# A decode layer that streams its cache: sixteen-row loads, a staggered first chunk of w_down, and a store that all engines wait for

## The chip, the cores and the metric

The program runs on one core of one Trainium2 chip. The time is device time in microseconds of one execution; before the change the median of three runs is 1310.91 us. All profile rows are of one further, profiled execution. In them PE is TensorE, PEld its weight loads, DVE VectorE, ACT ScalarE, POOL GpSimd and SP SyncE; a q behind the name marks the engine's sequencer, which issues the DMAs. Times in rows count from the first instruction.

## What is computed

One token goes through an attention block over a cache of 65,536 positions and then through a bilinear feed-forward block. Everything is float32.

```python
# x (1,1,512); 32 query heads, 8 key/value heads, Dh 128, Sk 65536; F 1792
q = (layernorm(x) @ wq).reshape(32, 128)
p = softmax(q . k_cache[h // 4] * 128 ** -0.5)       # per query head
h = x + concat(p . v_cache[h // 4]) @ wo
hn = layernorm(h)
out = h + ((hn @ w_gate) * (hn @ w_up)) @ w_down
```

K and V are 268 MB each; all weights together are 27.3 MB.

## The kernel before, in words

All work of the engines is written out by hand with semaphores. Two slots in SBUF, `slots[0]` (slot_a) and `slots[1]` (slot_b), of 128 partitions by 64 KiB, take turns. The query weights `wq` (8 MiB) go into slot_a and the first tile of K into slot_b (L107, L108). After that, for each of the eight key/value heads, four tiles of K and four tiles of V of 8 MiB each follow (L130). SP issues each when TensorE has finished with the tile that was two earlier in the same order, which the counter `c_pe` tells it. TensorE multiplies the tiles (L276 for scores, L301 for the weighted sum of V). VectorE and ScalarE do the maximum, the exponentials and the copies out of PSUM.

At the start ACT issues the load of x (L105) into `x_col`, 128 rows of four elements. VectorE normalises it (L176 to L188) with two small sums over partitions on TensorE (L247, L248), and TensorE multiplies it with wq (L255) once slot_a is full. `psm` is a bank of PSUM that these small results share.

At the end the slots receive `wo` in two pieces (L139, slot_b) and w_gate and w_up (L142, L145, slot_a). w_down has a place of its own, `wd_t`, of 128 rows by 14 chunks of 512 elements, 2 KiB a row and chunk. It comes in five loads whose bounds in chunks are `WD_CUTS` (L149), and each has a semaphore. TensorE waits for w_down's pieces in order (L402) and adds four matmuls for each chunk (L407). VectorE then copies the sum into `y` (L411), SP stores four of y's rows, one for each quarter of the output (L412), and SP alone waits for the store (L414). All loads but x's are issued by SP, in the order of the code, without waits of their own between the pieces of w_up and w_down.

Of the kernel before, what the change touches and what calls it, by code (L numbers as in the profile page):

```python
# [15 lines left out]
KT = D // P  # L16
# [7 lines left out]
SMALL = 17408  # L24
SLOT_A, SLOT_B, SLOT_C = 65536, 131072, 196608
WO_CUT = 6 * REP * D
WU_CUTS = (0, 2, 3, 4)
WD_CUTS = (0, 4, 8, 11, 13, 14)


class Counter:
# [8 lines left out]
        return self.n  # L40


def body(nc, xc, kT, v, wq, wo, wg, wu, wd, out):
# [21 lines left out]
    x_col, xd, xq, hq = (sb(n, P, KT) for n in ("x_col", "xd", "xq", "hq"))  # L65
    eps_t, sel_1 = sb("eps_t", P, 1), sb("sel_1", P, 1)
    sel_h, sel_b, sel_q = sb("sel_h", P, REP), sb("sel_b", P, 16), sb("sel_q", P, 4)
    stat = sb("stat", P, 16)
# [17 lines left out]
    pva, psm = ps("pva"), ps("psm")  # L86

    slot_sem = [nc.alloc_semaphore("in_a"), nc.alloc_semaphore("in_b")]
    sem_x, sem_out = nc.alloc_semaphore("in_x"), nc.alloc_semaphore("out")
    tail_sem = [nc.alloc_semaphore(f"in_w{i}") for i in range(12)]  # L90
    dve_pe, act_pe = nc.alloc_semaphore("dve_pe"), nc.alloc_semaphore("act_pe")
    c_pe, c_dve, c_act, c_pool = (Counter(nc, n) for n in ("c_pe", "c_dve", "c_act", "c_pool"))
# [4 lines left out]
        out=ident, in_=ident, compare_op=ALU.not_equal, fill=1.0, base=0,  # L97
# [13 lines left out]
    Q_ROWS, Q_COLS = 3, 5  # L111
    BASE, PER_HEAD = 5, 16
    K_DONE, MT, MB, T_DONE, V_DONE, PL, PO = 1, 5, 6, 7, 11, 15, 16

    def pe_at(h, k):
# [18 lines left out]
    tail = iter(tail_sem)  # L134
    wo_sems, wu_sems, wd_sems = [], [], []
# [10 lines left out]
            wu_sems[-1][1], 16)  # L146
    for lo, hi in zip(WD_CUTS, WD_CUTS[1:]):
        wd_sems.append((lo, next(tail)))
        SP.dma_start(wd_t[:, lo * D:hi * D], wd[:, lo * D:hi * D]).then_inc(wd_sems[-1][1], 16)  # L149


    def dve(ins):
        return c_dve.up(ins)
# [4 lines left out]
    dve(DVE.memset(mean_m, 1.0 / D))  # L158
    dve(DVE.memset(ones, 1.0))
    for t in (pva, psm):  # L160
        dve(DVE.memset(t, 0.0))
# [14 lines left out]
    t = dve(DVE.tensor_reduce(out=s1, in_=x_col, axis=AX.X, op=ALU.add)._wait_ge(sem_x, 16))  # L176
    ln_in = t
    dve(DVE.tensor_copy(x_pad[:, :, 0], x_col))
    t = dve(DVE.tensor_copy(mean, psm[:, 0:1])._wait_ge(c_pe.sem, 1))
# [5 lines left out]
    ln_std = c_act.up(ACT.activation(  # L185
        std, psm[:, 1:2], AF.Sqrt, bias=eps_t[:, 0:1], scale=1.0)._wait_ge(c_pe.sem, 2))
    t = dve(DVE.reciprocal(rstd, std)._wait_ge(c_act.sem, ln_std))
    xn_done = dve(DVE.tensor_scalar(  # L188
        out=xn_pad[:, :, 0], in0=xd, scalar1=rstd, scalar2=None, op0=ALU.mult)._wait_ge(
# [5 lines left out]
    for i in range(2):  # L195
        t = dve(DVE.tensor_copy(
            q_all[:, 4 * i:4 * i + 4, :],
            ptp[i][:, 0:16].rearrange("p (r j) -> p j r", j=4)))
    dve_to_pe(DVE.tensor_copy(q_pad[:, 28:28 + REP], q_all[:, 0, :])._wait_ge(c_dve.sem, t))

    for h in range(HKV):
        for n in range(NT):
            t = dve(DVE.tensor_reduce(  # L203
                out=mx[:, n:n + 1], in_=psc[n], axis=AX.X, op=ALU.max)._wait_ge(
                    c_pe.sem, pe_at(h, K_DONE + n)))
        dve_to_pe(DVE.tensor_reduce(out=m1, in_=mx, axis=AX.X, op=ALU.max)._wait_ge(c_dve.sem, t))
        t = dve(DVE.tensor_reduce(
            out=m_row, in_=psm[0:1, 0:P].rearrange("p (g h) -> p h g", h=REP), axis=AX.X,
            op=ALU.max)._wait_ge(c_pe.sem, pe_at(h, MT)))
# [3 lines left out]
            out=nbias, in0=psm[:, 128:129], scalar1=-SCALE, scalar2=None,  # L213
# [7 lines left out]
        for n in range(NT):  # L221
# [18 lines left out]
    def pe(ins):  # L240
        return c_pe.up(ins)

    def take(sem, n=1):
        PE.sem_inc(sem, -n).wait_op(sem, n, "sem-ge")  # L244

    PE.wait_ge(c_dve.sem, ln_in)
    pe(PE.matmul(psm[:, 0:1], mean_m, s1, start=True, stop=True))  # L247
    pe(PE.matmul(psm[:, 1:2], mean_m, s2, start=True, stop=True)._wait_ge(c_dve.sem, ln_sq))  # L248
    PE.wait_ge(c_dve.sem, xn_done)
    take(slot_sem[0], 16)  # L250
    for i in range(2):
        for k in range(KT):
            for j in range(4):
# [3 lines left out]
                    start=(k == 0), stop=(k == KT - 1))  # L257
    assert pe(ins) == Q_ROWS
    PE.wait_ge(c_dve.sem, q_rows)
    for i in range(2):  # L260
        for r in range(REP):
            ins = PE.matmul(
                ptp[i][:, 4 * r:4 * r + 4], q_row[i][:, r * P:(r + 1) * P], sel_q,
                start=True, stop=True)
        t = pe(ins)
    assert t == Q_COLS == BASE

    with PE.Fori(0, HKV):
        take(dve_pe)
        for n in range(NT):  # L270
# [14 lines left out]
            start=True, stop=True))  # L285
# [113 lines left out]
    wd_at = dict(wd_sems)  # L399
    for c in range(NC):  # L400
        if c in wd_at:
            PE.wait_ge(wd_at[c], 16)  # L402
        if c == 8:
            PE.wait_ge(c_dve.sem, fp1_done)
        for j in range(4):
            o = c * D + j * P
            ins = PE.matmul(  # L407
                pd[32 * j:32 * j + 32, 0:P], f_pad[:, c, :], wd_t[:, o:o + P],
                start=False, stop=(c == NC - 1))
    pd_done = pe(ins)  # L410
    y_done = dve(DVE.tensor_copy(y, pd[:, 0:P])._wait_ge(c_pe.sem, pd_done))  # L411
    SP.dma_start(out, y[0:P:32, :])._wait_ge(  # L412
        c_dve.sem, y_done).then_inc(sem_out, 16)
    SP.wait_ge(sem_out, 16)  # L414


# [32 lines left out]
```

## Time and profile before

| | before |
|---|---|
| median of 3 runs | 1310.91 us (1310.81 to 1310.94) |
| the profiled execution, as timed | 1310.62 us |
| its span, first to last instruction | 1309.3 us |
| mean granted TensorE clock | 0.735 |
| bytes moved by DMA | 564.81 MB, 431 GB/s over the span |
| DMA packets | 11107, of which 1364 under 512 B |
| load of wq, issue to landing | 21.9 us |
| load of x, issue to landing | 12.3 us |

The page gives busy time by engine, 40 equal slices of the span, the DMA queues, the chain of work that ended last, the costliest groups of instructions and the DMA issues. The views behind it give the same for any stretch: windows (busy time of each engine in a stretch, then TensorE's clock, the busy share of the 16 DMA engines and GB/s, where a packet is booked whole where it starts), the timeline, the waits, and the DMA of one stretch. A share over 1 in a short window comes from that booking.

### The profile page before, as it was taken

To read this page: it belongs to the slowest core of one execution; us is meant where nothing else is said; L and a number is where in the kernel's file an instruction comes from. 1 tells how busy PE (TensorE), PEld (TensorE's weight loads), DVE (VectorE), ACT (ScalarE), POOL (GpSimd) and SP (SyncE) were. 2 spreads that over 40 slices of the span, in tenths; PEclk is the share of its full clock that TensorE was granted. 3 is DMA by queue.
4 is the path that set the end of the run, shared out by engine and by line. 5 is a ranking of instruction groups with operands and counts; after the bars stand their busy time and mean duration, and the time that the engine had idled before them with its cause. 6 is when DMAs were issued, how large, how long until landed. Compare 5 with 4: busy or idle time off the path is not lost. (4 is left out here: it accounts for less than half of the span.)

```text
span 1309.3 us, 9941 instructions
## 1 busy us (share of the span) xinstructions
PE 669.7 (51%) x4692; PEld 201.7 (15%) x4692; DVE 69.2 (5%) x177; ACT 28.0 (2%) x72; POOL 2.6 (0%) x13
## 2 busy tenths in 40 slices
PE   3447445455535534554543654555464554456357
PEld 1112011121111101110110211111111111112013
DVE  1001000010001000010000100001000100001000
ACT  0000000000000000000000000000000000000000
POOL 0000000000000000000000000000000000000000
PEclk9677676667678777767767767776876776776678
DMA  9999999999999999999999999999999999999998
GB/s 417 431 431 441 425 443 427 436 428 436 434 432 444 424 442 428 436 428 436 428 438 444 425 440 428 438 428 436 428 438 440 428 440 428 438 428 436 428 430 356
DMA packets 11107, 564.81 MB, mean 431 GB/s; under 512 B 1364, under 2 KB 1368, under 8 KB 2008
## 3 DMA queue, kind: packets, MB, share of 16 engines
q1 hardware_dynamic: 10952, 564.67, 99.6%
q8 instruction: 7, 0.11, 0.0%
q14 instruction: 4, 0.03, 0.0%
q10 hardware_dynamic: 144, 0.00, 0.0%
HBM read 564.66 MB, written 0.00 MB: 431 GB/s over the span
## 5 line engine op out<-in xcount | busy, mean ns | idle before, releaser
L276 PE MATMUL psc<-slot_a,q_pad 128*32 128x512 f32 x1024 | 147.6, 741 | 164.5 <-PEq L244 164.5
L301 PE MATMUL pva<-slot_a,pt 128*16 128x512 f32 x1024 | 146.2, 735 | 162.0 <-PEq L244 162.0
L276 PE MATMUL psc<-slot_b,q_pad 128*32 128x512 f32 x1024 | 145.7, 733 | 143.0 <-PEq L244 143.0
L301 PE MATMUL pva<-slot_b,pt 128*16 128x512 f32 x1024 | 147.1, 739 | 105.4 <-PEq L244 105.4
L276 PEld LDWEIGHTS psc<-slot_a,q_pad 128*32 128x32 f32 x1024 | 40.7, 133 | 271.4 <-issue 271.4
L276 PEld LDWEIGHTS psc<-slot_b,q_pad 128*32 128x32 f32 x1024 | 40.2, 132 | 242.0 <-issue 242.0
L301 PEld LDWEIGHTS pva<-slot_a,pt 128*16 128x16 f32 x1024 | 34.4, 112 | 273.7 <-issue 273.7
L301 PEld LDWEIGHTS pva<-slot_b,pt 128*16 128x16 f32 x1024 | 34.7, 113 | 213.7 <-issue 213.7
L203 DVE TENSOR_REDUCE mx<-psc 128x1 f32<-128x512 f32 x32 | 22.1, 692 | 582.9 <-PE psc L276 582.9
L216 ACT ACTIVATE sc<-psc,nbias 128x512 f32<-128x512 f32 x32 | 21.6, 686 | 1159.5 <-DVE nbias L212 1159.5
L230 DVE COPY o_row<-pva 128x512 f32<-128x512 f32 x8 | 5.5, 692 | 552.8 <-PE pva L301 552.8
L291 PE MATMUL ptp<-ident,sc 128*128 128x128 f32 x128 | 28.2, 387 | 10.2 <-PEq L244 9.8
L291 PEld LDWEIGHTS ptp<-ident,sc 128*128 128x128 f32 x128 | 21.1, 198 | 14.8 <-issue 14.1
L222 DVE COPY pt<-ptp 128x512 f32<-128x512 f32 x32 | 22.1, 692 | 20.6 <-PE ptp L291 20.5
L255 PE MATMUL psc<-slot_a,xn_pad 128*32 128x512 f32 x64 | 10.0, 792 | 7.4 <-PEq L244 7.4
L311 PE MATMUL ptp<-sel_b,o_row 128*128 128x4 f32 x64 | 8.2, 252 | 4.7 <-PEq L244 4.7
L326 PE MATMUL psc<-slot_b,o_pad 128*32 128x512 f32 x64 | 8.4, 686 | 3.7 <-DMA slot_b<-in_wo 3.7
L366 PE MATMUL psc<-slot_a,hn_pad 128*32 128x448 f32 x64 | 8.2, 653 | 3.0 <-DMA slot_a<-in_wg 1.7
L311 PEld LDWEIGHTS ptp<-sel_b,o_row 128*128 128x128 f32 x64 | 7.7, 191 | 5.2 <-issue 5.2
L247 PE MATMUL psm<-stat,mean_m 128*128 128x1 f32 x2 | 0.6, 362 | 13.3 <-DVE stat L176 13.3
L281 PE MATMUL psm<-ident,m 128*1 128x128 f32 x8 | 2.2, 269 | 8.7 <-PEq L244 8.7
L216 ACT ACTIVATION_READ_ACCUMULATOR sc<-psc,nbias 128x1 f32 x32 | 6.5, 203 | 0.0
(95 smaller groups left out, 72.5 us busy)
## 6 DMA issues: line engine op xcount, KB each, us to landing
slot_b<-in_wo SPq DMA_DIRECT2D x1, 6144.0 KB, 23.6
slot_a<-in_wg SPq DMA_DIRECT2D x1, 3584.0 KB, 18.7
slot_b<-in_wo SPq DMA_DIRECT2D x1, 2048.0 KB, 28.1
wd_t<-in_wd SPq DMA_DIRECT2D x2, 1024.0 KB, 28.9
slot_a<-in_wu SPq DMA_DIRECT2D x1, 1792.0 KB, 22.6
slot_a<-in_wu SPq DMA_DIRECT2D x2, 896.0 KB, 25.2
wd_t<-in_wd SPq DMA_DIRECT2D x1, 768.0 KB, 31.3
wd_t<-in_wd SPq DMA_DIRECT2D x1, 512.0 KB, 32.1
```

The costliest lines, as they stand in the source:

```text
L203: t = dve(DVE.tensor_reduce(out=mx[:, n:n + 1], in_=psc[n], axis=AX.X, op=ALU.max)._wait_ge(c_pe.sem, pe_at(h, K_DONE + n)))
L216: e = ACT.activation(sc[n], psc[n], AF.Exp, bias=nbias[:, 0:1], scale=SCALE, accum_out=sums[:, n:n + 1])
L222: dve_to_pe(DVE.tensor_copy(pt[n].rearrange("p g b h -> p b g h"), ptp[n % 2].rearrange("p (b g h) -> p b g h", b=4, h=REP))._wait_ge(c_pe ...
L230: dve_to_pe(DVE.tensor_copy(o_row, pva)._wait_ge(c_pe.sem, pe_at(h, V_DONE + NT - 1)))
L255: ins = PE.matmul(psc[i][32 * j:32 * j + 32, :], xn_pad[:, k, :], slots[0][:, o:o + 512], start=(k == 0), stop=(k == KT - 1))
L276: ins = PE.matmul(psc[n][32 * j:32 * j + 32, :], q_pad[:, 28 - 4 * rs:60 - 4 * rs], slots[s][:, o:o + 512], start=(rs == 0), stop=(rs == 7))
L281: pe(PE.transpose(psm[0:1, 0:P], m1, ident))
L291: ins = PE.transpose(ptp[n % 2][:, b * P:(b + 1) * P], sc[n][:, b * P:(b + 1) * P], ident)
L301: ins = PE.matmul(pva[32 * j:32 * j + 16, :], pt[n][:, 8 * j + rs, :, :].rearrange("p b h -> p (b h)"), slots[s][:, o:o + 512], start=(n = ...
L311: ins = PE.matmul(ptp[1][:, 0:REP], o_row[:, b * P:(b + 1) * P], sel_b[:, 4 * b:4 * b + 4], start=(b == 0), stop=(b == 3))
L326: ins = PE.matmul(attn[32 * j:32 * j + 32, :], o_pad[:, kk, :], wo_t[:, kk * D:(kk + 1) * D], start=(kk < 4), stop=(kk >= HKV * REP - 4))
L366: ins = PE.matmul(acc[32 * j:32 * j + 32, :FJ], hn_pad[:, k, :], wgu_t[:, o:o + FJ], start=(k == 0), stop=(k == KT - 1))
```

## The change

Four things change. The load of wq is cut into rows 0 to 15 and rows 16 to 127. x arrives as 16 rows of 32 elements in `x_row`; four small matmuls with columns of the identity turn it into PSUM in the layout of `x_col`, and VectorE copies it there. The first of w_down's 14 chunks is taken out of its load of four chunks and is loaded by 16 loads of its own, of 1, 2, 3 and so on to 15 rows and one of 8, on one semaphore; the other three chunks of that load follow. The store takes every eighth row of `y`, 16 rows, of which the host keeps four; and all five engines wait for it.

```diff
+WQ_ROWS = (0, 16, P)
+WD_STRIPS = (*range(1, 16), 8)
...
-    x_load = ACT.dma_start(x_col, xc)
-    x_load.then_inc(sem_x, 16)
-    SP.dma_start(slots[0], wq).then_inc(slot_sem[0], 16)
+    ACT.dma_start(x_row, xr).then_inc(sem_x, 16)
+    for lo, hi in zip(WQ_ROWS, WQ_ROWS[1:]):
+        SP.dma_start(slots[0][lo:hi, :], wq[lo:hi, :]).then_inc(slot_sem[0], 16)
...
     for lo, hi in zip(WD_CUTS, WD_CUTS[1:]):
         wd_sems.append((lo, next(tail)))
+        if lo == 0:
+            hi, row = lo + 1, 0
+            for n in WD_STRIPS:
+                SP.dma_start(wd_t[row:row + n, 0:D], wd[row:row + n, 0:D]).then_inc(
+                    wd_sems[-1][1], 16)
+                row += n
+            assert row == P
+            lo, hi = 1, WD_CUTS[1]
+            wd_sems.append((lo, next(tail)))
         SP.dma_start(wd_t[:, lo * D:hi * D], wd[:, lo * D:hi * D]).then_inc(wd_sems[-1][1], 16)
...
-    t = dve(DVE.tensor_reduce(out=s1, in_=x_col, axis=AX.X, op=ALU.add)._wait_ge(sem_x, 16))
-    ln_in = t
+    t = dve(DVE.tensor_copy(x_col, psm[:, 4:4 + KT])._wait_ge(c_pe.sem, X_COLS))
+    ln_in = dve(DVE.tensor_reduce(
+        out=s1, in_=x_col, axis=AX.X, op=ALU.add)._wait_ge(c_dve.sem, t))
...
+    PE.wait_ge(c_pool.sem, 2)
+    PE.wait_ge(c_dve.sem, psm_clear)
+    PE.wait_ge(sem_x, 16)
+    for j in range(4):
+        ins = PE.matmul(
+            psm[32 * j:32 * j + 32, 4:4 + KT], x_row, ident[0:16, j:j + 13:4],
+            start=True, stop=True)
...
-    take(slot_sem[0], 16)
+    take(slot_sem[0], 16 * (len(WQ_ROWS) - 1))
...
-            PE.wait_ge(wd_at[c], 16)
+            PE.wait_ge(wd_at[c], 16 if c else 16 * len(WD_STRIPS))
...
-    SP.dma_start(out, y[0:P:32, :])._wait_ge(
-        c_dve.sem, y_done).then_inc(sem_out, 16)
-    SP.wait_ge(sem_out, 16)
+    SP.dma_start(out, y[0:P:8, :])._wait_ge(c_dve.sem, y_done).then_inc(sem_out, 16)
+    for eng in (SP, PE, DVE, ACT, POOL):
+        eng.wait_ge(sem_out, 16)
```

On SP the program starts with these rows before the change (rows and elements of each load; c_pe is TensorE's counter):

```order
L107 DMA slot_a<-in_wq 128x16384 [waits barrier_Pool_Activation_PE_DVE_SP_release]
L108 DMA slot_b<-in_kT 128x16384
L130 DMA slot_a<-in_kT 128x16384 [waits c_pe]
L130 DMA slot_b<-in_kT 128x16384 [waits c_pe]
L130 DMA slot_a<-in_kT 128x16384 [waits c_pe]
```

and with these after it:

```order
L110 DMA slot_a<-in_wq 16x16384 [waits barrier_Pool_Activation_PE_DVE_SP_release]
L110 DMA slot_a<-in_wq 112x16384
L111 DMA slot_b<-in_kT 128x16384
L133 DMA slot_a<-in_kT 128x16384 [waits c_pe]
L133 DMA slot_b<-in_kT 128x16384 [waits c_pe]
```

One load has become two, ahead of the first tile of K. The end of SP's program, from w_up on, reads before:

```order
L145 DMA slot_a<-in_wu 128x3584
L145 DMA slot_a<-in_wu 128x1792 x2
L149 DMA wd_t<-in_wd 128x2048 x2
L149 DMA wd_t<-in_wd 128x1536
L149 DMA wd_t<-in_wd 128x1024
L149 DMA wd_t<-in_wd 128x512
L412 DMA out_y<-y 4x128 [waits c_dve]
```

and after:

```order
L148 DMA slot_a<-in_wu 128x3584
L148 DMA slot_a<-in_wu 128x1792 x2
L155 DMA wd_t<-in_wd 1x512
L155 DMA wd_t<-in_wd 2x512
...
L155 DMA wd_t<-in_wd 15x512
L155 DMA wd_t<-in_wd 8x512
L161 DMA wd_t<-in_wd 128x1536
L161 DMA wd_t<-in_wd 128x2048
L161 DMA wd_t<-in_wd 128x1536
L161 DMA wd_t<-in_wd 128x1024
L161 DMA wd_t<-in_wd 128x512
L433 DMA out_y<-y 16x128 [waits c_dve]
```

Sixteen short loads now stand ahead of the five wide ones. On VectorE, the path from x into the layer norm begins before with

```order
L176 TENSOR_REDUCE stat<-x_col 128x1 [waits in_x]
L178 COPY x_pad<-x_col 128x4
L179 COPY stat<-psm 128x1 [waits c_pe]
L180 TENSOR_SCALAR xd<-x_col,stat 128x4 [waits c_dve]
L182 TENSOR_TENSOR xq<-xd 128x4 [waits c_dve]
L183 TENSOR_REDUCE stat<-xq 128x1 [waits c_dve]
```

and after with

```order
L188 COPY x_col<-psm 128x4 [waits c_pe]
L189 TENSOR_REDUCE stat<-x_col 128x1 [waits c_dve]
L191 COPY x_pad<-x_col 128x4
L192 COPY stat<-psm 128x1 [waits c_pe]
L193 TENSOR_SCALAR xd<-x_col,stat 128x4 [waits c_dve]
L195 TENSOR_TENSOR xq<-xd 128x4 [waits c_dve]
```

VectorE's wait for the load of x has become a wait for TensorE, which now waits for that load itself.

More of the change, by code (lines that the diff above doesn't have):

```diff
@@ L40, in up, with body @@
         return self.n
-def body(nc, xc, kT, v, wq, wo, wg, wu, wd, out):
+def body(nc, xr, kT, v, wq, wo, wg, wu, wd, out):
     PE, DVE, ACT, POOL, SP = nc.tensor, nc.vector, nc.scalar, nc.gpsimd, nc.sync
@@ L65, in body @@
     x_col, xd, xq, hq = (sb(n, P, KT) for n in ("x_col", "xd", "xq", "hq"))
+    x_row = sb("x_row", 16, 32)
     eps_t, sel_1 = sb("eps_t", P, 1), sb("sel_1", P, 1)
@@ L101, in body @@
         pool_done = c_pool.up(POOL.memset(t, 0.0))
[L105 to L107 removed]
+    ACT.dma_start(x_row, xr).then_inc(sem_x, 16)
+    for lo, hi in zip(WQ_ROWS, WQ_ROWS[1:]):
+        SP.dma_start(slots[0][lo:hi, :], wq[lo:hi, :]).then_inc(slot_sem[0], 16)
     SP.dma_start(slots[1], kT[0, 0]).then_inc(slot_sem[1], 16)
[L111 to L112 removed]
+    X_COLS, MEAN, SQ, Q_ROWS, Q_COLS = 1, 2, 3, 4, 6
+    BASE, PER_HEAD = 6, 16
     K_DONE, MT, MB, T_DONE, V_DONE, PL, PO = 1, 5, 6, 7, 11, 15, 16
@@ L160, in body @@
     for t in (pva, psm):
-        dve(DVE.memset(t, 0.0))
+        psm_clear = dve(DVE.memset(t, 0.0))
     eps_done = dve(DVE.memset(eps_t, EPS))
@@ L175, in body @@
     s1, mean, s2, std, rstd = (stat[:, k:k + 1] for k in range(5))
-    t = dve(DVE.tensor_reduce(out=s1, in_=x_col, axis=AX.X, op=ALU.add)._wait_ge(sem_x, 16))
-    ln_in = t
+    t = dve(DVE.tensor_copy(x_col, psm[:, 4:4 + KT])._wait_ge(c_pe.sem, X_COLS))
+    ln_in = dve(DVE.tensor_reduce(
+        out=s1, in_=x_col, axis=AX.X, op=ALU.add)._wait_ge(c_dve.sem, t))
     dve(DVE.tensor_copy(x_pad[:, :, 0], x_col))
-    t = dve(DVE.tensor_copy(mean, psm[:, 0:1])._wait_ge(c_pe.sem, 1))
+    t = dve(DVE.tensor_copy(mean, psm[:, 0:1])._wait_ge(c_pe.sem, MEAN))
     t = dve(DVE.tensor_scalar(
@@ L185, in body @@
     ln_std = c_act.up(ACT.activation(
-        std, psm[:, 1:2], AF.Sqrt, bias=eps_t[:, 0:1], scale=1.0)._wait_ge(c_pe.sem, 2))
+        std, psm[:, 1:2], AF.Sqrt, bias=eps_t[:, 0:1], scale=1.0)._wait_ge(c_pe.sem, SQ))
     t = dve(DVE.reciprocal(rstd, std)._wait_ge(c_act.sem, ln_std))
@@ L244, in take @@
         PE.sem_inc(sem, -n).wait_op(sem, n, "sem-ge")
+    PE.wait_ge(c_pool.sem, 2)
[5 more added lines that the diff above has]
+            start=True, stop=True)
+    assert pe(ins) == X_COLS
     PE.wait_ge(c_dve.sem, ln_in)
@@ L431 @@
     arrays = {
-        "xc": lay(A_x, KT, P, perm=(1, 0)),
+        "xr": lay(A_x, 16, 32),
         "kT": lay(A_k_cache, HKV, NT, P, TPC, DH, perm=(0, 1, 4, 3, 2)).reshape(HKV, NT, P, CK),
@@ L444 @@
     ]
-    out = nc.dram_tensor("out_y", (4, P), F32, kind="ExternalOutput").ap()
+    out = nc.dram_tensor("out_y", (16, P), F32, kind="ExternalOutput").ap()
     body(nc, *args, out)
     r = run_bass_kernel_spmd(nc, [{f"in_{n}": a for n, a in arrays.items()}], core_ids=[0])
-    return np.asarray(r.results[0]["out_y"]).reshape(1, 1, D)
+    return np.asarray(r.results[0]["out_y"])[0:16:4].reshape(1, 1, D)
```

## Prediction

> **What bounds the kernel now.** I read the page first, its shares by engine and its line of DMA slices, then the stretches by window, then the chain of work that ended last, and last the first and the final microseconds one row at a time.
>
> ```profile
> PE 669.7 (51%) x4692; PEld 201.7 (15%) x4692; DVE 69.2 (5%) x177; ACT 28.0 (2%) x72; POOL 2.6 (0%) x13
> q1 hardware_dynamic: 10952, 564.67, 99.6%
> 300.00:1250.00 950.00, 482.52 (x3338) 139.95 (x3334) 45.83 (x108) 16.72 (x48) 0.00 (x0) 0.73 1.00 434
> DMA to landing us min/median/max: 28.4/29.3/30.8
> ```
>
> TensorE is idle half the time; the queue of SP's loads fills 99.6% of all 16 DMA engines' time. The third row (engines' busy time, TensorE clock, DMA share, GB/s) holds a share of 1.00 at 434 GB/s for 950 us, so one DMA engine moves 434/16 = 27.1 GB/s, and a row of 64 KiB, of which each 128-row load gives every engine eight, takes 65.536/27.1 = 2.42 us. The last row is for the 8 MiB loads of L130: 29.3 us from issue to landing, against 8 x 2.42 = 19.3 us of moving, so each is issued some 10 us before the engines reach it. Inside the loop, then, nothing but bytes counts, and the change moves no byte there. What can move is how early the engines start, whether they stay fed at full rate, how evenly they end, and what comes behind the last byte:
>
> ```profile
> 1271.91 29.90 DMA wd_t<-in_wd
> 1301.85 4.21 PE pva L407 x80
> 1306.06 0.02 issue
> 1306.08 0.29 DVE y L411
> 1306.40 0.65 SPq L412 DMA_DIRECT2D out_y<-y  x1
> SPq L414 <- DMA out_y<-y: 2.2, 1, 2.2
> ```
>
> The chain runs from w_down's pieces through TensorE's last matmuls, the copy to y and the store; SP waits 2.2 us for that store, and the span ends at 1309.3. The profiled execution took 1310.62 us, 1.3 us around its span; the median of the runs is 1310.91, 0.29 above it. I work out a difference against the profiled execution and put it on the median.
>
> **Query weights in two loads, x as 16 rows.** Windows of 0.2 us show the engines' start (the last two figures are DMA share and GB/s; a packet counts where it starts):
>
> ```profile
> 1.70:1.90 0.20, 0.00 (x0) 0.00 (x0) 0.14 (x2) 0.00 (x0) 0.20 (x1) 1.00 3.06 986
> 1.90:2.10 0.20, 0.00 (x0) 0.00 (x0) 0.20 (x1) 0.00 (x0) 0.20 (x1) 1.00 5.80 1969
> 2.10:2.30 0.20, 0.00 (x0) 0.00 (x0) 0.20 (x3) 0.00 (x0) 0.20 (x1) 1.00 0.89 328
> 2.30:2.50 0.20, 0.00 (x0) 0.00 (x0) 0.20 (x3) 0.09 (x1) 0.20 (x1) 1.00 4.40 1639
> 2.50:2.70 0.20, 0.00 (x0) 0.00 (x0) 0.20 (x3) 0.20 (x1) 0.20 (x3) 1.00 0.81 328
> ```
>
> 986 x 0.2 = 197 KB is three rows of 64 KiB; the five windows hold 3, 6, 1, 5 and 1, all 16 engines, spread over some 0.9 us. If the first load only has one row for each engine, the late ones may start with the early ones. The gain lies between 0 (the spread has another cause) and 0.9 us for the last engine. It is part of the spread at the end, below, and is counted there. The second piece of wq costs one more issue on SP, 0.43 us by the row of 1272.38 below, while the first row of each engine still moves for 2.42 us: nothing.
>
> ```profile
> 13.07 0.16 DVE L176 TENSOR_REDUCE stat<-x_col 128x1 f32<-128x4 f32 x1 [9.28 <-DMA x_col<-in_xc]
> 13.28 0.59 PE L247 MATMUL psm<-stat,mean_m 128*128 128x1 f32 x2 [13.28 <-DVE stat L176]
> 15.88 0.23 DVE L188 TENSOR_SCALAR xn_pad<-xd,stat 128x4 f32<-128x4 f32 x1
> 22.79 9.97 PE L255 MATMUL psc<-slot_a,xn_pad 128*32 128x512 f32 x64 [7.44 <-PEq L244]
> 42.11 3.64 PE L276 MATMUL psc<-slot_b,q_pad 128*32 128x512 f32 x16 [5.56 <-PEq L244]
> ```
>
> x is normalised by 16.11, and TensorE then stands until wq is there at 22.7. The four new matmuls and the copy out of PSUM cost at most 4 x 0.59 + 0.16 = 2.5 us by the nearest rows. Even if x lands no earlier than now, it is ready at 18.6, four microseconds early. Cost 0; without that cover 2.5 us. The K loads behind it have the same kind of slack: the first is used at 42.1, and the next was issued at 32.8.
>
> **w_down's first chunk in 16 loads.** They stand on SP between w_up and the rest of w_down:
>
> ```profile
> 1271.91 0.42 SPq L149 DMA_DIRECT2D wd_t<-in_wd  x1
> 1272.38 0.43 SPq L149 DMA_DIRECT2D wd_t<-in_wd  x1
> 1272.85 2.32 SPq L149 DMA_DIRECT2D wd_t<-in_wd  x1
> 1275.21 6.03 SPq L149 DMA_DIRECT2D wd_t<-in_wd  x1
> 1288.39 6.28 PE L366 MATMUL psc<-slot_a,hn_pad 128*32 128x448 f32 x48 [1.67 <-DMA slot_a<-in_wg]
> 1296.99 0.96 PE L366 MATMUL psc<-slot_a,hn_pad 128*32 128x448 f32 x8 [1.18 <-DMA slot_a<-in_wu]
> ```
>
> A free issue takes 0.42 to 0.43 us; the store's, with four rows, takes 0.65. Sixteen cost 6.7 to 10.4 us: SP is through them by about 1282, while w_gate and w_up keep the engines fed until 1297. The rows of 2.32 and 6.03 us say that SP is held when too much is queued. When the last one went out, at 1281.2, an engine had some 8 (w_gate) + 24 (w_up) + 40 (w_down) = 72 rows ahead of it. With that as the limit, the new list (8 + 24 + up to 16 + 40 = 88 on the fullest engine) is out once 16 rows are gone, after w_gate and w_up's first piece, near 1293; counting completions as entries too, near 1296. Both are before its rows are needed. Cost 0, with the rival below if the limit is another.
>
> What the pieces do to the end is read here:
>
> ```profile
> 1303.40:1303.80 0.40, 0.40 (x12) 0.04 (x6) 0.00 (x0) 0.00 (x0) 0.00 (x0) 0.50 0.75 287
> 1303.80:1304.20 0.40, 0.40 (x10) 0.37 (x13) 0.00 (x0) 0.00 (x0) 0.00 (x0) 0.50 0.48 195
> 1304.20:1304.60 0.40, 0.40 (x13) 0.38 (x8) 0.00 (x0) 0.00 (x0) 0.00 (x0) 0.50 0.40 154
> 1304.60:1305.00 0.40, 0.40 (x16) 0.20 (x6) 0.00 (x0) 0.00 (x0) 0.00 (x0) 0.50 0.33 128
> 1305.00:1305.40 0.40, 0.40 (x20) 0.38 (x16) 0.00 (x0) 0.00 (x0) 0.00 (x0) 0.67 0.07 26
> ```
>
> The engines end over two microseconds: the shares add up to 2.03 x 0.4 = 0.81 us of all 16, so ends that were even would come at 1303.4 + 0.8 = 1304.2, and 1.1 us is the most there is. A row of the first chunk is 2 KiB, 0.08 us at 154/(0.40 x 16) = 24 GB/s. If a load of n rows goes to n engines, always from the same end of the list, then loads of 1 to 15 rows and one of 8 give the first engine 16 rows and the last none instead of 8 each: plus and minus 0.64 us. That helps if the engines served first end first, and hurts by up to 0.64 us if not. With the earlier start I take -0.4, bounds -1.1 and +0.65. [...]
>
> **The store and the waits behind it.** Sliced finely (1307.6 to the end, 40 slices of 0.04 us):
>
> ```profile
> DMA  0000004000007000000000000000000000000000
> GB/s 0 24 12 0 0 0 193 0 0 0 0 0 193 12 0 0 0 0 0 0 0 0 0 0 0 0 0 0 0 0 0 0 0 0 0 0 0 0 0 0
> q14 instruction: 2, 0.02, 3.0%
> L130 SPq DMA_DIRECT2D slot_a<-in_kT x16: 327/328/328, 32.8 to 1153.6; - x16
> ```
>
> Three of the store's four rows (24 and 12 GB/s) move at 1307.65, the fourth half a microsecond later, behind instruction fetches of 8 KiB at 1307.87 and 1308.13. These come 1.8 us after TensorE and VectorE run out of work (1306.06, 1306.37). If both engines now wait for the store, the fetches should move behind it and 0.5 us goes; a 16-row store may also issue in 0.33 instead of 0.65 us, like a 128-row load. Against that stand 12 more rows, any of which can be late. I take -0.6, bounds -0.8 and +0.5. The waits themselves hold no queue, but whatever TensorE and VectorE do behind the program has so far been covered by the 3.2 us (1309.3 - 1306.06) in which SP was still busy; if it is longer than what SP does, it now adds. Between 0 and 3.2 us; I take +0.4, near the row of 0, because only 1.3 us lie around the span at all. The sum is -0.4 - 0.6 + 0.4 = -0.6 us: 1310.0 against the profiled execution, **1310.3** on the median. The ends (-1.9 and +4.35) put its own range at 1309.0 to 1315.3; so long a tail behind the program is unlikely, so I close it at 1313.5.
>
> **Rivals.**
>
> *Sixteen neighbouring rows share a path (slower).* The trace has no load of fewer than 128 rows, only a 27.1 GB/s that may belong to the engine or to the group of partitions it writes. If it belongs to the group, with eight partitions to each as in the even 128-row loads, then wq's first 16 rows send all 16 engines at a few groups: two if a group is one run of eight rows, four if it is two runs of four. Four engines to one group take 4 x 2.42 = 9.7 us for one row each, 7.3 us lost on every engine, and since engines are the bound nothing gives it back. Eight to one group lose 7 x 2.42 = 16.9 us. The 112 rows behind can add to the first case: when I step 16 engines through seven neighbouring rows each at four to a group, the slowest ends about 17 us late. So +7.3 to +17, 1318 to 1328, some 1321 in the middle; it decides as soon as four engines on one group are slower than one. For it speaks that an even 434 GB/s needs every engine kept apart from the others; against it, that no row shows any engine slowed by where it writes. [...]
>
> *SP is held by a count of loads, not by rows (slower).* The stall of 2.32 us ends as the first piece of wo lands; it would fit a limit of about nine loads in flight. Then from the sixth small load on one goes out per landing, at 1297 seven small loads and five large ones are still to be issued, and the engines stand for 7 x 0.43 us and the 1.1 us from issue (0.73) to first packets (1.8): +4, 1314.3. The stall of 6.03 us, which ends 1.3 us after wo's second piece has landed, speaks against it.
>
> *Ends even out wholly (faster).* -1.1, -0.8 and no cost of the waits, with the start brought forward by the other engines' 0.7: -2.6, 1308.3.
>
> **How the numbers follow.** Forecast 0.50; shared path 0.40, as it has no row against it but none for it; count of loads 0.04; even ends 0.06. A measurement of this kernel tells about 0.2%, 2.6 us, from no change. The forecast falls within that but for 0.02 of its slow end; half of the even ends are beyond it on the fast side; shared path and count of loads are slower. That gives faster 0.03, same 0.51, slower 0.46. The range reaches from 1308.6, halfway from the forecast's 1309.0 to the even ends, to 1327.5, almost the top of the shared path, and leaves out about a tenth.
>
> **What would show it.** Start: the windows at 1.7 to 2.7 should hold 16 rows by 2.1, and from 3 to 20 us a share of 1.00 at 434 GB/s. With a shared path the GB/s there falls towards 109 for ten microseconds and wq lands at 30 us or later instead of 22.7. Strips: the last load of w_down should be issued before 1297, and the shares at the end fall within a microsecond; with a count limit a gap opens at 1297. Store: no instruction fetch between the store's rows, SP's wait of 2.2 us nearer 1.7. What would prove me wrong is any lasting fall of GB/s while fewer than 128 rows move, or a time around the span that grows by more than a microsecond.

## The result and the profile after

The changed kernel takes 1332.14 us (median of 4 runs, 1331.78 to 1333.02) against 1310.86 of the kernel before on the same chip: 21.3 us more, ratio 1.0163 with a 95% interval of 1.0146 to 1.0181. It is 1.6% slower; the forecast was 1310.3, and the time lies 4.6 us above the top of the range, 1327.5. The profiled execution took 1333.02 us with a span of 1331.2.

I read it in the order of the prediction's last part. First the stretches by window, the last two figures being DMA share and GB/s; of the kernel before:

```profile
3.00:13.00 10.00, 0.00 (x0) 0.00 (x0) 0.72 (x4) 0.69 (x1) 0.20 (x2) 1.00 0.97 420
13.00:30.00 17.00, 8.38 (x44) 3.02 (x48) 1.33 (x8) 1.54 (x2) 0.00 (x0) 1.00 1.00 432
30.00:50.00 20.00, 13.03 (x104) 5.42 (x100) 1.71 (x5) 0.00 (x0) 0.00 (x0) 0.74 0.97 420
```

and of the changed one:

```profile
3.00:13.00 10.00, 0.00 (x0) 0.00 (x0) 0.72 (x4) 0.69 (x1) 0.19 (x2) 1.00 0.55 105
13.00:30.00 17.00, 1.45 (x12) 1.22 (x12) 1.50 (x9) 1.54 (x2) 0.00 (x0) 1.00 0.97 247
30.00:50.00 20.00, 5.02 (x24) 1.38 (x28) 0.00 (x0) 0.00 (x0) 0.00 (x0) 1.00 0.96 301
300.00:1250.00 950.00, 486.29 (x3338) 149.46 (x3334) 45.88 (x108) 16.70 (x48) 0.00 (x0) 0.73 1.00 434
```

In the second and the third stretch the engines are as busy as before (0.97 and 0.96), but they move 247 instead of 432 and 301 instead of 420 GB/s: their packets take longer. (420 - 105) x 10 + (432 - 247) x 17 + (420 - 301) x 20 = 8.7 MB are missing by 50 us, which at 434 GB/s is 20 us. Between 300 and 1250 us nothing differs (1.00 and 434 in both). The page's line for the queue of SP's loads still says 99.6%:

```profile
q1 hardware_dynamic: 11248, 564.67, 99.6%
```

So a share near 1 does not say that bytes move at full rate (0.97 stands beside 247 GB/s here and beside 420 in the kernel before); GB/s has to be read beside it. The loss falls on the first load. Time from issue to landing of the two pieces of wq, the 16-row piece first and the 112-row piece last:

```profile
DMA to landing us min/median/max: 11.9/27.8/43.6
```

Before, the one load took 21.9. In the rows of the timeline below, which are a part of it, the first is x, the fourth is TensorE's first matmul on wq, and the last three are at the end.

```profile
13.04 0.28 PE L263 MATMUL psm<-ident,x_row 16*32 16x4 f32 x8 [13.04 <-DMA x_row<-in_xr]
13.38 0.16 DVE L188 COPY x_col<-psm 128x4 f32<-128x4 f32 x1 [9.59 <-PE psm L263]
16.40 0.23 DVE L201 TENSOR_SCALAR xn_pad<-xd,stat 128x4 f32<-128x4 f32 x1
44.98 1.94 PE L276 MATMUL psc<-slot_a,xn_pad 128*32 128x512 f32 x8 [29.12 <-PEq L257]
1293.03 5.97 SPq L155 DMA_DIRECT2D wd_t<-in_wd  x16
1299.04 14.11 SPq L161 DMA_DIRECT2D wd_t<-in_wd  x5
1329.31 0.60 SPq L433 DMA_DIRECT2D out_y<-y  x1
```

x is normalised at 16.63 instead of 16.11, and TensorE then stands until 44.98 instead of 22.79: 22.2 us. The store goes out at 1329.31 instead of 1306.40, 22.9 us later, so the tail adds 0.7. The engines' start and SP's wait for the store:

```profile
1.70:1.90 0.20, 0.00 (x0) 0.00 (x0) 0.14 (x2) 0.00 (x0) 0.20 (x1) 1.00 10.38 1311
1.90:2.10 0.20, 0.00 (x0) 0.00 (x0) 0.20 (x1) 0.00 (x0) 0.20 (x1) 1.00 13.78 1638
2.10:2.30 0.20, 0.00 (x0) 0.00 (x0) 0.20 (x3) 0.00 (x0) 0.20 (x1) 1.00 5.36 655
2.30:2.50 0.20, 0.00 (x0) 0.00 (x0) 0.20 (x3) 0.09 (x1) 0.20 (x1) 1.00 10.45 1311
2.50:2.70 0.20, 0.00 (x0) 0.00 (x0) 0.20 (x3) 0.20 (x1) 0.20 (x3) 1.00 2.64 328
```

```profile
SPq L435 <- DMA out_y<-y: 1.2, 1, 1.2
```

In rows of 64 KiB the first five windows hold 4, 5, 2, 4 and 1, against 3, 6, 1, 5 and 1: the start is spread as before. A packet's whole time counts in the window where it starts, so a share of 10.38 says at once that these rows will be long: 10.38 x 0.2 x 16 / 4 = 8.3 us each, against 3.06 x 0.2 x 16 / 3 = 3.3 before. SP's wait for the store fell from 2.2 to 1.2, but the time around the span rose from 1.3 to 1.8.

### The profile page after: what moved, and what is told of

Its sections match the earlier page's. It is cut to its first block, busy times and chain, and to the rows that moved or that the text cites. A ratio compares the mean times of both kernels' runs of the same rounds, so it can differ in the third digit from the quotient of the medians.

```text
span 1331.2 us, 9980 instructions
## 1 busy us (share of the span) xinstructions
PE 670.9 (50%) x4700; PEld 212.7 (16%) x4700; DVE 69.4 (5%) x178; ACT 28.0 (2%) x72; POOL 2.6 (0%) x13
## 3 DMA queue, kind: packets, MB, share of 16 engines
q1 hardware_dynamic: 11248, 564.67, 99.6%
## 5 line engine op out<-in xcount | busy, mean ns | idle before, releaser
L297 PEld LDWEIGHTS psc<-slot_b,q_pad 128*32 128x32 f32 x1024 | 49.6, 131 | 232.8 <-issue 227.7
L312 PEld LDWEIGHTS ptp<-ident,sc 128*128 128x128 f32 x128 | 21.2, 197 | 14.7 <-issue 14.1
## 6 DMA issues: line engine op xcount, KB each, us to landing
slot_b<-in_wo SPq DMA_DIRECT2D x1, 6144.0 KB, 23.8
slot_a<-in_wu SPq DMA_DIRECT2D x1, 1792.0 KB, 22.8
```

The lines of the kernel that those rows point to most:

```text
L297: ins = PE.matmul(psc[n][32 * j:32 * j + 32, :], q_pad[:, 28 - 4 * rs:60 - 4 * rs], slots[s][:, o:o + 512], start=(rs == 0), stop=(rs == 7))
L312: ins = PE.transpose(ptp[n % 2][:, b * P:(b + 1) * P], sc[n][:, b * P:(b + 1) * P], ident)
```

## Experiments

**Which part.** The change with wq in one load, and the kernel before with nothing but wq in two loads.

```diff
 e1_wq_whole, against the changed kernel:
-WQ_ROWS = (0, 16, P)
+WQ_ROWS = (0, P)
 e2_wq_split_only, against the kernel before:
+WQ_ROWS = (0, 16, P)
...
-    SP.dma_start(slots[0], wq).then_inc(slot_sem[0], 16)
+    for lo, hi in zip(WQ_ROWS, WQ_ROWS[1:]):
+        SP.dma_start(slots[0][lo:hi, :], wq[lo:hi, :]).then_inc(slot_sem[0], 16)
...
-    take(slot_sem[0], 16)
+    take(slot_sem[0], 16 * (len(WQ_ROWS) - 1))
```

> The changed kernel with wq in one load of 128 rows again; everything else of the change stays. If cutting wq costs the time (shared path): wq lands at 22.7 us instead of 44.8, and the time falls by 21 to 22 us to 1310 to 1312; x lands near 5 us instead of 13. If the sixteen short loads of w_down or the waits at the end carry the loss, it stays above 1325.

> The kernel before with one edit: wq in rows 0 to 15 and rows 16 to 127. Shared path: wq lands near 44.8 us as in the changed kernel, time 1331 to 1333 (+21 to +22). If the loss needs the rest of the change: at most 1315.

The first took 1311.84 us (10 runs; before 1310.62, ratio 1.0009, 0.9999 to 1.0019), the second 1331.82 (4 runs; ratio 1.0159, 1.0142 to 1.0176). The cut of wq is 21.2 us by itself; all the rest together is 1.2, with an interval that includes no change. In the first run wq lands at 22.8 us again, as expected, and x at 8.3, where I had said near 5; in the second wq lands at 44.65.

**Does the place of the rows set the rate?** The kernel before with wq in eight loads of 16 rows: neighbouring rows in one run, in the other every eighth partition (the host lays the rows of each load side by side, so that what is read stays in one piece). Here and in the runs on wq below, the lines shown stand in place of the one load of wq, and TensorE waits for as many loads as there are.

```diff
 e3_wq_near16, with the loop of e2_wq_split_only:
+WQ_ROWS = tuple(range(0, P + 1, 16))
 e4_wq_spread16:
+    for i in range(8):
+        SP.dma_start(slots[0][i:P:8, :], wq[16 * i:16 * i + 16, :]).then_inc(slot_sem[0], 16)
```

> The kernel before with wq in eight loads of 16 neighbouring rows each. Shared path, four engines to a group in every load: each load takes 8.4 to 9.7 us, wq lands at 69 to 81 us, time 1357 to 1369. If rows that lie side by side in HBM are what is slow, or any load of 16 rows: the same here, and the next kernel tells it apart. If only the issue of more loads costs: wq lands at 23 to 26 us, time 1311 to 1314.

> As the kernel with eight loads of 16 neighbouring rows, each load reading the same 64 KiB rows side by side in HBM, but written to every eighth partition (the rows are stored in that order beforehand). Shared path by groups of two runs of four partitions 32 apart: 16 such partitions lie in eight groups, two engines each, 4.84 us a row, wq lands near 42 us, time near 1330. If the source or the mere number of 16 rows is slow: the same as with neighbouring rows, 1357 to 1369.

The first took 1365.6 us, the second 1331.49 (one run each; before 1310.62). Windows of the run with neighbouring rows:

```profile
30.00:40.00 10.00, 0.00 (x0) 0.00 (x0) 0.00 (x0) 0.00 (x0) 0.00 (x0) 1.00 0.94 105
40.00:50.00 10.00, 0.00 (x0) 0.00 (x0) 0.00 (x0) 0.00 (x0) 0.00 (x0) 1.00 0.94 105
```

and of the run with every eighth partition:

```profile
20.00:30.00 10.00, 0.00 (x0) 0.00 (x0) 0.00 (x0) 0.00 (x0) 0.00 (x0) 1.00 1.00 210
30.00:40.00 10.00, 0.00 (x0) 0.00 (x0) 0.00 (x0) 0.00 (x0) 0.00 (x0) 1.00 1.03 210
```

A quarter and a half of 434. The same bytes in as many loads of as many rows go at two rates, 105 and 210 GB/s, by where they are written. An estimate from these rates: if the 434 GB/s of loads of 128 rows are 16 groups of partitions at 27.1 each, then 16 neighbours reach 105/27.1 = 3.9 groups and every eighth partition 210/27.1 = 7.7. One arrangement that would give this is groups of two runs of four neighbouring partitions, the second run 32 further on: 16 neighbours lie in 4 of 16 such groups and every eighth partition in 8, a quarter and a half. It is this estimated grouping that the following runs try.

**The 112 rows.** Four runs of the kernel before ask why the larger piece was slow too: rows 0 to 15 and then seven loads of every seventh row, which are the rows that 16 blocks of seven would write at the same time; the same with those rows side by side in what is read; two halves; and sixteen loads of eight rows, every fourth partition of 32.

```diff
 e9_wq_every7 (e11_every7_src: the same partitions, read from rows side by side):
+    SP.dma_start(slots[0][0:16, :], wq[0:16, :]).then_inc(slot_sem[0], 16)
+    for i in range(16, 23):
+        SP.dma_start(slots[0][i:P:7, :], wq[i:P:7, :]).then_inc(slot_sem[0], 16)
 e10_wq_halves, with the loop of e2_wq_split_only:
+WQ_ROWS = (0, 64, P)
 e12_wq_eight4:
+    for b in range(0, P, 32):
+        for a in range(b, b + 4):
+            SP.dma_start(slots[0][a:b + 32:4, :], wq[a:b + 32:4, :]).then_inc(slot_sem[0], 16)
```

> The kernel before with wq's rows 0 to 15 in one load, and rows 16 to 127 in seven loads of every seventh row, so that at any moment the engines write the same rows as if the one load of 112 rows were cut into blocks of seven neighbouring rows. If that load is so cut and the groups are not two runs of four partitions: wq lands near 44.8 us again, time near 1332. If the groups are right, most of these rows lie in groups of their own, wq lands at 33 to 39 us, time 1322 to 1328, and the load of 112 rows must be cut in another way.

> The kernel before with wq in two loads of 64 rows. Shared path, blocks of four neighbouring rows to an engine: partitions 0 to 63 are eight groups, two engines to each, so each half takes 19.3 us, wq lands near 42 us, time near 1330. If rows went round the engines one by one, four to a group: 77 us, time near 1368. If 64 rows were spread over all 16 groups: 22.7 us, 1311.

> As the kernel with rows 0 to 15 and seven loads of every seventh row, with the same partitions written at the same moments, but each load's 16 rows lie side by side in HBM (stored in that order beforehand) instead of seven rows apart. If only the written partitions decide: wq lands at 44.4 us again, time 1331 to 1332. If reading rows seven apart was slow: 33 to 39 us, time 1322 to 1328.

> The kernel before with wq in 16 loads of 8 rows, every fourth row of 32, so that each of eight engines has a group to itself; the first eight loads write partitions 0 to 63, the last eight 64 to 127. If only a shared group slows an engine: all 16 loads take 2.4 us each, the eighth lands near 22 us, the sixteenth near 41 us, time near 1330, as eight engines carry all of wq. If an engine has its full rate only into the group it writes in 128-row loads: the last eight take 4.8 us each or more, wq lands at 60 us or later, time 1348 or more.

They took 1331.75, 1332.14, 1332.02 and 1342.39 us (one run each; before 1310.48, 1310.48, 1310.53 and 1310.53). The seven loads of every seventh row have their last row down at 44.4 us, like the 112-row load (44.65 alone), and so they do with the reading changed (44.3): a 112-row load behaves as 16 blocks of seven neighbouring rows, and what counts is where it writes. With groups that are right and independent of each other I had expected 33 to 39 us; so one of the two is wrong. Windows of the two halves:

```profile
20.00:30.00 10.00, 0.00 (x0) 0.00 (x0) 0.00 (x0) 0.00 (x0) 0.00 (x0) 1.00 1.01 210
30.00:40.00 10.00, 0.00 (x0) 0.00 (x0) 0.00 (x0) 0.00 (x0) 0.00 (x0) 1.00 1.02 210
```

64 neighbouring rows get half the rate, so by the estimate they reach 210/27.1 = 7.7, that is eight groups; had the second run of a group lain 64 further on, they would have reached all 16. The loads of eight rows show how a good case looks, and then a bad one:

```profile
15.00:20.00 5.00, 0.00 (x0) 0.00 (x0) 0.00 (x0) 0.00 (x0) 0.00 (x0) 1.00 0.99 419
20.00:25.00 5.00, 0.00 (x0) 0.00 (x0) 0.00 (x0) 0.00 (x0) 0.00 (x0) 1.00 1.50 419
25.00:30.00 5.00, 0.00 (x0) 0.00 (x0) 0.00 (x0) 0.00 (x0) 0.00 (x0) 1.00 1.00 210
```

A load of eight rows goes to one half of the engines (from 45 to 55 us the share is 0.49 at 210 GB/s, with wq's last loads still moving); the other half went on to the first K tile. While the loads wrote partitions 0 to 63, the rows that start between 16.6 and 21.3 us took 2.42 to 2.45 us in both halves; eight rows four partitions apart, with a second run 16 further on, would have met in pairs, so that grouping is out too; of a second run 16, 32 or 64 further on, 32 is left. When the loads came to partitions 64 to 127, at 23 us, all sixteen engines fell to 4.3 to 5.1 us a row, which fits if the other half writes its part of a 128-row load there. I had overlooked the K tile, and neither of the two times that I had worked out came.

So the estimated grouping fits these rates, and what fails is that groups are independent. With blocks of seven, by that grouping, a pair of engines meets in one group or in two groups at a time, and every other engine has a group to itself. The trace's single packets show what the other engines did meanwhile:

```
changed kernel, rows of 64 KiB in order of start, 16 at a time (start us: us each), and the pairs that meet by the grouping
  16-row piece    1.8-2.7: 7.5-9.1, four engines to a group
  112-row piece   9.3-11.2: 5.1-6.0, two pairs                15.3-16.3: 4.8-4.9, two pairs
                  20.2-21.1: 3.0-3.5, two at 4.9, one pair    23.6-25.9: 3.6-3.9, two at 4.4, one pair
                  27.3-29.7: 4.4-4.9, two pairs               31.7-34.4: 4.7-4.9, two pairs
                  36.6-39.1: 4.5-4.8, two pairs
```

In the kernel before, every row of wq behind an engine's first took 2.42 to 2.46 us. Here engines that by the grouping share with nobody are slowed too, and by the number of pairs: with one pair the fourteen others took 3.0 to 3.9 us, with two pairs all sixteen took 4.4 or more. The same steps stand out in e2, e9 and e11 (2.9 to 3.9 us against 4.0 to 6.0). No run changes the number of pairs alone, so this is read from traces and not tested. The last two of this series put one pair among eight engines, and one pair beside a K tile that by the grouping shares no group with it.

```diff
 e13_one_pair:
+    for a in range(5):
+        SP.dma_start(slots[0][a:a + 40:5, :], wq[a:a + 40:5, :]).then_inc(slot_sem[0], 16)
+    SP.dma_start(slots[0][40:P, :], wq[40:P, :]).then_inc(slot_sem[0], 16)
 e15_pair_among_16:
+    for lo, n in ((0, 7), (56, 9)):
+        for a in range(lo, lo + n):
+            SP.dma_start(slots[0][a:a + 7 * n + 1:n, :], wq[a:a + 7 * n + 1:n, :]).then_inc(slot_sem[0], 16)
```

> Kernel before, but query weights in five loads of eight rows (every fifth of 40 partitions) and one of the 88 rows left. By the grouping that the runs so far show (partitions p and p + 32 within a half share a group of four plus four), in the first two loads one pair of the eight engines shares a group (partitions 0 and 35, then 1 and 36) and six engines have a group of their own; in the last three loads two pairs share. Theory A (groups are independent): in the first loads six engines take about 2.42 us a row and two 4.84 us, so that the eight engines that write at that time run mostly at their full rate. Theory B (an engine held up at a busy group holds up others that use the same way): all eight take about 4.8 us a row from the first load on. The time itself, 1325 to 1345 us, doesn't tell them apart; the time of each row does.

> Kernel before, but query weights in sixteen loads of eight rows: seven at every seventh row of partitions 0 to 55, then nine at every ninth of 56 to 127. As in the run with eight rows at every fourth row, such loads go to one half of the sixteen engines, while the other half starts the first K tile at about 12 us. There the engines each had a group of their own and moved 419 GB/s at 15 to 20 us. Here one pair of the eight shares a group in six of the first seven loads. Theory A (groups are independent): at 15 to 20 us only the pair is slow, six engines and the eight of the K tile run on: 350 to 420 GB/s. Theory B (a shared group holds up all that write at the time): about 210 to 260 GB/s from the moment that the K tile starts.

They took 1363.87 and 1347.9 us (one run each; before 1310.88 and 1310.53). The first lies above the 1325 to 1345 that I had expected. Small loads keep half the engines from wq, so that the single rows tell more than these times. The trace's single packets, rows of 64 KiB, give (start us: us each):

```
e13, the eight engines of the small loads, and who came after
  2.3-2.9: six at 2.62-3.16, two at 4.21 and 4.53    5.0-5.4: the six at 2.42-2.68
  6.5-7.4: the two go on and eight others begin, 4.07-5.09
  7.7-7.9: the six, 4.43-4.63; then, to 17.5, all 4.97-5.11
e15, small loads (partitions 0 to 55) and K tile
  small loads, alone   5.7-10.8: 2.8-4.6
  small loads          12.2-13.6: 2.42-2.95   17.2-19.2: 3.13-3.24, two at 4.70 and 4.99
  K tile               15.7-16.0: 2.70-2.74   18.4-18.7: 3.16-3.17   21.6-21.8: 4.0-4.1
  both                 25.6-26.2: 4.83-5.00, one 5.45
```

In e13 the theory of independent groups held while eight engines wrote: until others joined in at 6.5 us, the pair alone was slow. (By the grouping the second load's pair is partitions 6 and 36, not 1 and 36, and only the third load has two pairs; the rows up to 5.4 us don't hang on that.) What came after doesn't tell, since the eight more engines had then begun on the load of 88 rows or the K tile. The windows of e15:

```profile
15.00:20.00 5.00, 0.00 (x0) 0.00 (x0) 0.00 (x0) 0.00 (x0) 0.00 (x0) 1.00 1.15 380
20.00:25.00 5.00, 0.00 (x0) 0.00 (x0) 0.00 (x0) 0.00 (x0) 0.00 (x0) 1.00 0.99 249
```

380 lies in what I had given for independent groups, but the rows say otherwise: beside a pair at 4.70 and 4.99, the other engines of the small loads took 3.13 to 3.24 us a row, and all eight engines on the K tile, which by the grouping shares no group with the small loads until these reach partition 64, took 3.16, where beside the loads without a pair (e12) they took 2.42. The small loads of e15 alone took 2.8 to 4.6, too, where those of e12 alone took 2.42 to 2.50 (5.6 to 11 us). The 4.0 to 4.1 of the K tile's next rows can't be used so: they end at 25.6 or later, and the small loads reach partition 64 and beyond from 23.8 on. So engines that write elsewhere were held up beside a pair, though in degrees, to 3.16 us from 2.42 and not at once to half rate. Why six engines in e13 escaped it stays open; no run shows by what path the engines hold each other up.

**The small parts.** The kernel before with the 16 loads of w_down's first chunk alone; with the 16-row store alone; with all engines waiting, the store at four rows; with both; and, last, with x as 16 rows and all engines waiting.

```diff
 e5_strips_only:  the 16 loads of 1 to 15 and 8 rows, and their waits, as in the change
 e6_store16:
-    SP.dma_start(out, y[0:P:32, :])._wait_ge(
-        c_dve.sem, y_done).then_inc(sem_out, 16)
+    SP.dma_start(out, y[0:P:8, :])._wait_ge(c_dve.sem, y_done).then_inc(sem_out, 16)
...
 e7_waits (e8_store16_waits: with the lines of e6 too):
-    SP.wait_ge(sem_out, 16)
+    for eng in (SP, PE, DVE, ACT, POOL):
+        eng.wait_ge(sem_out, 16)
 e14_x_and_waits: the lines of e7, and x_row, its four matmuls and its copy as in the change
```

> The kernel before with one edit: w_down's first chunk in the sixteen loads of 1 to 15 and 8 rows. If short neighbouring rows share a path here too: GB/s falls from 430 to 300 to 350 for some three microseconds while the loads run, the ends stay as spread as before, +0.8 to +1.2 us. If they only even out the ends: -0.3 to -0.6 us and no such fall.

> The kernel before with one edit: the store takes 16 rows of y instead of four, SP alone waits. If the 16-row form itself lands sooner: SP's wait behind the issue (2.2 us before) falls to 1.2 to 1.7 us and the time by 0.5 to 1.0 us. If only the instruction fetches behind the other engines' ends delayed it: one of the 16 rows still meets a fetch, wait 2.0 to 2.3 us, time the same within 0.2 us.

> The kernel before with one edit: all engines wait for the store of four rows. If the fetches delay the store's fourth row: the row comes with the others, SP's wait falls by 0.4 to 0.5 us. What the engines do behind the program is no longer covered, and the time around the span grows from 1.4 to 1.9 us: in sum 0 to +0.2 us. If that tail were free: -0.5 us.

> The kernel before with both edits at the end, 16 rows and all engines waiting. From the changed kernel: wait 1.1 to 1.2 us instead of 2.2, time around the span 1.8 to 2.0 instead of 1.4, in sum -0.4 to -0.6 us. If the two gains add up and the tail is free: -1.0 us or more.

> The parts of the change that cost nothing alone: x as 16 rows and all engines waiting for the store, which stays at four rows; query weights in one load, w_down's first chunk in one load. If the loss is all in the query weights and in the 16 loads of w_down, 1310.1 to 1310.6 us, ratio 0.9993 to 1.0000, not told from no change. If x as 16 rows costs by itself what the run with whole query weights still lost, 1311 to 1312 us.

| | us (runs) | before | ratio, 95% interval |
|---|---|---|---|
| 16 loads of w_down | 1312.14 (11) | 1310.67 | 1.0011, 1.0002 to 1.0020 |
| 16-row store | 1310.72 (11) | 1310.67 | 1.0000, 0.9991 to 1.0009 |
| all engines wait | 1310.31 (11) | 1310.67 | 0.9997, 0.9988 to 1.0006 |
| both of these | 1310.33 (11) | 1310.67 | 0.9997, 0.9988 to 1.0006 |
| x as 16 rows, all engines wait | 1310.34 (11) | 1310.88 | 0.9996, 0.9987 to 1.0005 |

Only the first interval excludes no change. Windows as the 16 loads move, first of the kernel before:

```profile
1295.00:1296.00 1.00, 0.81 (x8) 0.01 (x2) 0.00 (x0) 0.00 (x0) 0.00 (x0) 1.00 1.02 431
1296.00:1297.00 1.00, 0.01 (x1) 0.01 (x1) 0.00 (x0) 0.00 (x0) 0.00 (x0) 1.00 1.05 445
1297.00:1298.00 1.00, 0.95 (x8) 0.15 (x8) 0.00 (x0) 0.00 (x0) 0.00 (x0) 1.00 0.99 418
1298.00:1299.00 1.00, 0.36 (x4) 0.36 (x4) 0.81 (x2) 0.00 (x0) 0.00 (x0) 1.00 1.01 426
```

then of the run with the 16 loads:

```profile
1295.00:1296.00 1.00, 0.80 (x8) 0.00 (x0) 0.00 (x0) 0.00 (x0) 0.00 (x0) 1.00 1.08 353
1296.00:1297.00 1.00, 0.00 (x0) 0.00 (x0) 0.00 (x0) 0.00 (x0) 0.00 (x0) 1.00 1.01 293
1297.00:1298.00 1.00, 0.12 (x4) 0.12 (x8) 0.00 (x0) 0.00 (x0) 0.00 (x0) 1.00 1.05 303
1298.00:1299.00 1.00, 0.84 (x8) 0.04 (x5) 0.01 (x1) 0.00 (x0) 0.00 (x0) 1.00 0.99 371
```

1720 - 1320 = 400 KB less, 0.9 us at 434, again at a full share. The last piece of w_down lands at 1306.83 instead of 1305.55, and the ends are as ragged as they were. The single packets tell rows that were slowed from rows that are only shorter. A row of 2 KiB took 0.084 us in the kernel before, in the last piece of w_down, and 67 of the 128 rows of the short loads took 0.089 to 0.135. Of the 6 KiB rows of w_down's other three chunks, a load of all 128 partitions, 89 took 0.25 to 0.57 us instead of 0.234; 21 rows of w_up's last pieces were slowed too; in the kernel before none of these rows was. In sum the slowed rows cost 0.9 us on each of the 16 engines, the whole of what is missing. The shorter rows alone cost an engine 8 x (0.084 + 0.234 - 0.309) = 0.07 us.

The store, 1307.4 us to the end in 40 slices; first with 16 rows and SP alone waiting:

```profile
DMA  0000062110000600000000000000000000000000
GB/s 0 0 0 0 0 184 62 41 31 0 0 0 0 164 10 0 0 0 0 0 0 0 0 0 0 0 0 0 0 0 0 0 0 0 0 0 0 0 0 0
```

then with four rows and all engines waiting:

```profile
DMA  0000000100000000400000000000000000000060
GB/s 0 0 0 0 0 0 0 31 10 0 0 0 0 0 0 0 164 0 0 0 0 0 0 0 0 0 0 0 0 0 0 0 0 0 0 0 0 0 164 0
```

SP's waits for the two stores are, in the same order:

```profile
SPq L413 <- DMA out_y<-y: 2.2, 1, 2.2
SPq L415 <- DMA out_y<-y: 1.0, 1, 1.0
```

In the first, the two instruction fetches (in 184 and 164, a slice being 0.05 us) fall among the store's rows, the last row (10) moves only at 1308.1, and SP waits 2.2 us as before. In the second the store's rows are through before either fetch and SP waits 1.0. That is 1.2 less, where I had said 0.4 to 0.5: in the kernel before, the signals of three rows reach SP at 1308.05 and the fourth's only at 1309.24, so a row half a microsecond late cost more than its lateness, 1.19 us. Over the runs the span's median is 1308.5 instead of 1309.3, but 1.8 us lie around it instead of 1.4: of 0.8 us won inside, 0.4 come back outside, and the rest is too little to be told from no change. The run that leaves out the costly parts, 1310.34, is the best combination tried, and can't be told from the kernel before.

## Why the prediction was wrong

**The step that failed** is the sentence "The second piece of wq costs one more issue on SP ...: nothing", and with it the choice of the forecast, 0.50, over the rival "Sixteen neighbouring rows share a path", 0.40. The sentence rests on the first row of each engine moving for 2.42 us; in the 16-row piece it moved for 7.5 to 9.1, and the rows of the second piece for 3.0 to 6.0. The cut of wq measures +21.2 us by itself. I weighed the rival down because "no row shows any engine slowed by where it writes". That is no evidence: every load in the trace had all its rows spread evenly over the partitions, so no row could have shown it. What spoke for it, an even 434 GB/s over 16 engines, was the only thing the trace could say.

**The rival's first term was right in kind, and a little large.** Four groups for 16 rows were to give 4 x 2.42 = 9.7 us for the first row of each engine and 7.3 lost. The first rows took 8.5 us on average, at 105 GB/s, where before they took 3.0: 5.6 lost. The piece landed at 12.63. That there are four was a supposition that no row of the kernel before showed; the 105 GB/s of the run with 16 neighbouring rows put it at 105/27.1 = 3.9.

**Its second term was too small.** I let the 112 rows add 0 to 10 us by stepping engines through their blocks with only those in one group slowed. Their seven rows took an engine 31.3 us on average instead of 16.9, so the second piece cost 14.4, and the K tile's first rows another 0.8; with the 5.6 these are 20.8 us on the average engine, and wq lands 22.2 late on the last. The too small term is why the range ended at 1327.5. What failed is that groups are independent: beside a pair that by the grouping shares one, others were slower as well. e15 shows this for one pair, 3.16 us a row instead of 2.42, and in the load of 112 rows all sixteen engines took 4.4 us or more whenever two pairs met.

**w_down in 16 loads**: -0.4 was forecast, with bounds -1.1 and +0.65; it measures +1.5 (the interval of the ratio, 1.0002 to 1.0020, is +0.3 to +2.6). The sign was wrong: I counted how many rows each engine gets and at what speed 2 KiB move, not that loads of 1 to 15 neighbouring rows, by the grouping, sit in few groups too. The bounds' 0.64 us supposes that a load of n rows goes to n engines, always from the same end of the list; no run shows this, and what the run with the 16 loads showed instead is rows that took longer, 67 of 128 of 2 KiB 0.089 to 0.135 us against 0.084. The slowed packets account for 0.9 us of the 1.5, and the rest lies within the interval. That shared groups slowed them fits the estimate, but no run of its own tests it. That SP's issues cost nothing was right: the last was out by 1313.2 in the changed kernel, with w_up still moving. So the rival of a count of loads falls: SP issued 16 loads in 5.97 us without being held, and no gap opened.

**x** cost nothing: normalised half a microsecond later, 28 us before TensorE could use it, and 1310.34 in the run that has it without the cut. **The store** with 16 rows was forecast to win; by itself it measures +0.05 us, that is nothing, and its issue takes 0.59 us instead of 0.65, not the 0.33 that I had hoped for. **The waits** moved the fetches behind the store as said, and cost 0.4 outside the span against my +0.4; the two together measure -0.3 where I had -0.2, and neither can be told from nothing. **Even ends** did not come: in the run with the 16 loads the share falls over two microseconds as before (0.75, 0.81, 0.56, 0.17, 0.09 and 0.04 in steps of 0.4 us from 1304.2), and in the changed kernel the engines' start is spread as before.

The parts add up to 21.2 + 1.5 - 0.3 = 22.4 us against 21.3 measured; the intervals (2.2 us on the first alone) allow the difference.

## What to carry to other kernels

Where DMA engines are the bound, as here at a share of 1.00 and 434 GB/s, a load cut by rows is not free: the cut of wq cost 21.2 us. Give each load all 128 partitions and cut along the row, as w_down is cut in the kernel before, where none of its rows was slowed (each of 6 KiB took 0.234 us). By the estimated grouping, placing the rows of a shorter load so that all groups are reached evenly should do too, but only loads of eight rows were tried (2.42 to 2.45 us a row, up to partition 63). Read GB/s beside the busy share, because engines that count as busy moved bytes at a quarter of their rate for ten microseconds (share 0.94 at 105 GB/s, from 30 to 40 us in the run with neighbouring rows). And where the trace has no instance of the case that a change makes, the absence of a counterexample is not evidence; price the rival as if it were open.

## What the runs showed of the hardware that was not expected

- Loads of 16 rows of 64 KiB to neighbouring partitions moved at 105 GB/s, of 64 rows at 210, of 128 rows at 434, with the engines' share at 0.94, 1.01 and 1.00.
- Eight rows to partitions four apart took the eight engines that carry them 2.42 to 2.45 us each, as in a load of 128 rows, while the other eight carried the next load; this ended once they wrote partitions 64 to 127 (4.3 to 5.1 us on all sixteen).
- Beside loads of eight rows of which, by the estimated grouping, one pair shares a group, the eight engines that write elsewhere took 3.16 us a row instead of 2.42. In the load of 112 rows one pair left fourteen engines at 3.0 to 3.9 us, and two pairs brought all sixteen to 4.4 to 6.0.
- Rows of full 128-row loads that moved beside sixteen loads of few neighbouring rows took longer, 6 KiB as much as 0.57 us instead of 0.234.
- With two instruction fetches of 8 KiB among a store's rows at the program's end, the last row moved half a microsecond after the others and its signal came 1.2 later, and SP waited 2.2 us; a wait of all engines moved the fetches behind the store, SP waited 1.0, and 0.4 us more lay outside the span.
